# Retention and two MLPs in one launch: order of ScalarE's work in the opening, and the queue that reloads the low parts of x

## The chip, the cores and the metric

One core of a Trainium2 chip. The metric is the device time of one execution in microseconds (us), the median of the runs. TensorE is the matrix engine (PE in the profile's rows, PEld its weight loads), VectorE is DVE, ScalarE is ACT, GpSimd is POOL; SyncE (SP) has no arithmetic and only asks for transfers. ACTq and SPq in a row are these engines' sequencers asking for a transfer.

## What is computed

```python
# q, k, v: [4, 8, 768, 64]
for t in range(S):
    state = gamma * state + k[t] outer v[t]
    y[t] = scale * q[t] @ state
x = y as [3072, 512]
h = x @ w_in;  x = (h * cos(h)) @ w_out                 # first MLP, d_ff 2048
h = x @ w_in;  x = act(h) @ w_out                       # second MLP
```

act is h for h >= 1, 0 for h <= -1 and (h + 1)^2 / 4 between.

## The kernel before

All work is in one program whose instructions stand in the order written by hand: each engine runs its own in that order, and semaphores hold one engine for another. Every float operand of a matmul is split into a high part and a low part (names ending in h and l); a product is three matmuls: high by high, low by high, high by low.

The 3072 tokens are six blocks b of 512, d_ff is sixteen chunks j of 128. The first MLP goes in two passes: k=0 takes chunks 0 to 7 for all blocks, k=1 chunks 8 to 15. That makes 96 steps (k, b, j). In a step TensorE does `first` (L793: 12 matmuls, x by w_in, into a PSUM bank) and `second` of the step three before (L893: 12 matmuls, g by w_out). Between them stand, for each step, `Parts`: `rounded` on ScalarE (L842, into a tile r), `fraction` on VectorE (L847), `cosine` on ScalarE (L853), and, beside the next step's `rounded`, `product` on VectorE (L856), `high` on ScalarE (L861, gh) and `low` on VectorE (L869, gl). The sums of a block are copied into tiles `o` and stored to yT by SP (L925); these tiles `o` and the tiles r come out of one set of five.

**Weights are converted in between.** A class `Convert` takes a raw load of weights (raw<-in_w, L191, SP) through numbered stages: `one` and `two` on ScalarE (L204, L211: cf or f, and cs), `shift` and `sign` on VectorE (L223, L229), `four` on GpSimd (L238, the sum), `five` on ScalarE (L141: the high part wih, woh or whi), `six` on GpSimd (L144: the low part wil, wol). For the second MLP the results and sums of them (s, L287) go to DRAM as wp, by SP (L318). In the opening x and y in the code are lists of such conversions: x[1] makes wih and wil of chunk 1, y[1] woh and wol, x[2] the next wih.

**The opening.** While the attention of the first tokens still runs (`att`: scores L505, masks L575, decays of keys and queries L483 and L493, state updates L617 and L628, the output's parts `finish_high` L141 and `finish_low` L734), three steps of the first MLP are written out by hand in the function `opening(i, n)` (L1602), i = 0, 1, 2.

**x between the passes.** In pass 0 the parts of x are stored to DRAM (xTh, xTl). For pass 1 they are read back block by block into tiles xh and xl. `load_parts` (L762), called in the third step of the block before, writes down four pieces, two of xh and two of xl, 512 KB each; `fetch_x` (L771), called in every step between `first` and `second`, asks for up to two of the pieces, on SP. So xh is asked for in the step after `load_parts`, xl in the step after that; blocks b = 0 to 5 of pass 1 have four pieces each, 12 loads of xh and 12 of xl.

**Semaphores of transfers.** The transfers of SP and ScalarE share eight semaphores, DMAHW0 to DMAHW7, in turn; a transfer waits for the one that held its semaphore before. An engine that has come to a transfer that waits does nothing else until then.

## Time and profile before

| | us |
|---|---|
| median of three runs | 1064.48 (1064.04 to 1064.78) |
| the profiled execution, its own time | 1065.51 |
| its span, first to last instruction | 1063.7 |
| TensorE busy | 1054.7 |
| VectorE busy | 754.8 |
| ScalarE busy | 639.5 |
| GpSimd busy | 598.4 |

The mean granted TensorE clock is 0.999 of full speed. 1.8 us of the profiled execution lie outside its span. In the rows, a timeline's line joins neighbouring instructions of one kind (xcount): the first number is the start of the first, the second the time to the end of the last, and the bracket behind is the time for which the engine stood still before it and what ended that.

### The profile page before, as it was taken

To read this page: it belongs to the slowest core of one execution; us is meant where nothing else is said; L and a number is where in the kernel's file an instruction comes from. 1 tells how busy PE (TensorE), PEld (TensorE's weight loads), DVE (VectorE), ACT (ScalarE), POOL (GpSimd) and SP (SyncE) were. 2 spreads that over 40 slices of the span, in tenths; PEclk is the share of its full clock that TensorE was granted. 3 is DMA by queue.
4 is the path that set the end of the run, shared out by engine and by line. 5 is a ranking of instruction groups with operands and counts; after the bars stand their busy time and mean duration, and the time that the engine had idled before them with its cause. 6 is when DMAs were issued, how large, how long until landed. Compare 5 with 4: busy or idle time off the path is not lost.

```text
span 1063.7 us, 17827 instructions
## 1 busy us (share of the span) xinstructions
PE 1054.7 (99%) x6290; PEld 865.1 (81%) x6290; DVE 754.8 (71%) x1035; ACT 639.5 (60%) x1148; POOL 598.4 (56%) x520
## 2 busy tenths in 40 slices
PE   8999999999999999999999999999999999999998
PEld 6788888888888888888878888888888888888887
DVE  6858777887566446657475577778887787987875
ACT  4664344544366455657475677777667786666764
POOL 4844212221155377877885378965549885464550
PEclk9999999999999999999999999999999999999999
DMA  9697599898574699988988679898489899586642
GB/s 352 230 324 225 162 278 293 290 282 281 167 265 188 224 301 323 343 275 309 312 280 299 224 252 316 279 366 298 163 227 331 319 350 351 159 265 199 213 136 87
DMA packets 131705, 280.21 MB, mean 263 GB/s; under 512 B 14624, under 2 KB 41376, under 8 KB 131616
## 3 DMA queue, kind: packets, MB, share of 16 engines
q1 hardware_dynamic: 121968, 251.80, 70.6%
q10 hardware_dynamic: 9648, 27.27, 7.1%
q8 instruction: 50, 0.82, 0.3%
q14 instruction: 39, 0.32, 0.1%
HBM read 195.39 MB, written 83.62 MB: 262 GB/s over the span
## 4 chain that ended last, share of the span: by engine, by line
PE 84%; DMA 7%; POOL 4%; DVE 3%; issue 1%; ACT 1%; SPq 1%; POOLq 0%; ACTq 0%; DVEq 0%
PE b L1119 21%; PE y L1137 21%; PE b L893 19%; PE b L793 18%; DMA wp<-s 3%; PE b L661 2%; DMA yT<-o 1%; PE b L1253 1%; DMA qk<-in_qk 1%; POOL s L144 1%; PE b L537 1%; PE b L554 1%; DMA xl<-xTl 1%; POOL s L287 1%; DMA wp<-f 1%
## 5 line engine op out<-in xcount | busy, mean ns | idle before, releaser
L842 ACT ACTIVATE r<-b 128x512 int32<-128x512 f32 x96 | 56.8, 591 | 156.9 <-PE b L793 129.8
L847 DVE SCALAR_TENSOR_TENSOR r<-b,r 128x512 f32<-128x512 f32 x96 | 66.0, 687 | 109.6 <-ACT r L842 104.3
L1190 DVE TENSOR_TENSOR xh<-y,xh 128x1024 f32<-128x1024 f32 x86 | 105.1, 1222 | 30.6 <-PE y L1137 29.1
L238 POOL TENSOR_TENSOR cf<-cf,cs 128x512 int32<-128x512 int32 x40 | 51.6, 1290 | 131.9 <-DVE cf L229 93.9
L893 PE MATMUL b<-gh,wo 128*128 128x512 f32 x384 | 97.9, 389 | 0.0
L793 PE MATMUL b<-xh,wi 128*128 128x512 f32 x384 | 94.8, 389 | 0.0
L1310 POOL TENSOR_TENSOR ft<-r,f 128x512 f32<-128x512 f32 x23 | 29.8, 1296 | 114.1 <-PE y L1137 100.9
L1119 PE MATMUL b<-wih,wi 128*128 128x512 f32 x320 | 86.9, 389 | 0.0
L1190 DVE TENSOR_TENSOR xl<-y,xl 128x1024 f32<-128x1024 f32 x63 | 76.7, 1218 | 13.2 <-PE y L1137 13.2
L1137 PE MATMUL y<-gh,wo 128*128 128x512 f32 x276 | 85.0, 389 | 0.0
L893 PEld LDWEIGHTS b<-gh,wo 128*128 128x128 f32 x384 | 72.0, 188 | 15.2 <-ACT gh L861 0.2
L793 PEld LDWEIGHTS b<-xh,wi 128*128 128x128 f32 x384 | 72.1, 188 | 15.0
L893 PE MATMUL b<-gh,woh 128*128 128x512 f32 x192 | 76.9, 406 | 0.6 <-DVE xl L734 0.4
L861 ACT ACTIVATE gh<-b 128x512 fp32r<-128x512 f32 x96 | 57.0, 594 | 31.7 <-DVE b L856 31.5
L853 ACT ACTIVATE r<-r 128x512 f32<-128x512 f32 x96 | 60.7, 632 | 25.5 <-DVE r L847 25.3
L893 PE MATMUL b<-gh,wol 128*128 128x512 f32 x192 | 73.9, 390 | 0.0
L793 PE MATMUL b<-xh,wih 128*128 128x512 f32 x192 | 73.6, 396 | 0.2
L793 PE MATMUL b<-xh,wil 128*128 128x512 f32 x192 | 72.4, 390 | 0.0
L869 DVE TENSOR_TENSOR gl<-b,gh 128x512 fp32r<-128x512 f32 x96 | 65.7, 684 | 7.7 <-ACT gh L861 5.6
L1119 PEld LDWEIGHTS b<-wih,wi 128*128 128x128 f32 x320 | 60.0, 188 | 12.7 <-DVE gl L1162 0.3
L1137 PE MATMUL y<-wo,wo 128*128 128x512 f32 x276 | 70.0, 389 | 0.0
L1137 PE MATMUL y<-wi,wo 128*128 128x512 f32 x276 | 70.0, 389 | 0.0
(184 smaller groups left out, 2768.7 us busy)
## 6 DMA issues: line engine op xcount, KB each, us to landing
wi<-wp SPq DMA_DIRECT2D x66, 512.0 KB, 5.2
raw<-in_w SPq DMA_DIRECT2D x64, 512.0 KB, 6.6
wo<-wp SPq DMA_DIRECT2D x63, 512.0 KB, 5.5
wp<-whi SPq DMA_DIRECT2D x48, 256.0 KB, 4.3
wp<-s SPq DMA_DIRECT2D x32, 256.0 KB, 3.7
w<-cf ACTq DMA_DIRECT2D x26, 256.0 KB, 5.2
xTh<-xh ACTq DMA_DIRECT2D x12, 512.0 KB, 6.0
xTl<-xl ACTq DMA_DIRECT2D x12, 512.0 KB, 6.4
```

The lines of the kernel that those rows point to most:

```text
L238: nc.gpsimd.tensor_tensor(out=f, in0=f, in1=self.s, op=ALU.add)
L793: nc.tensor.matmul(out=h, lhsT=w[:, c * P:(c + 1) * P], rhs=x[:, c, :], start=(i == 0), stop=(i == len(terms) - 1),)
L842: nc.scalar.activation(out=self.r.bitcast(I32), in_=self.h, func=AF.Identity, scale=INV_2PI, bias=0.25)
L847: nc.vector.scalar_tensor_tensor(out=self.r, in0=self.h, scalar=INV_2PI, in1=self.r.bitcast(I32), op0=ALU.mult, op1=ALU.subtract,)
L853: nc.scalar.activation(out=self.r, in_=self.r, func=AF.Sin, scale=TWO_PI, bias=HALF_PI)
L861: nc.scalar.activation(out=self.gh, in_=self.h, func=AF.Copy)
L869: nc.vector.tensor_tensor(out=self.gl, in0=self.h, in1=self.gh.bitcast(F32), op=ALU.subtract)
L893: nc.tensor.matmul(out=acc[k, b][e], lhsT=w[:, s], rhs=g, start=(begin and i == 0), stop=(last and i == 2),)
L1119: nc.tensor.matmul(out=to, lhsT=w[:, c * P:(c + 1) * P], rhs=x, start=begin and n == 0, stop=n == len(terms) - 1, skip_group_check=not begin,)
L1137: nc.tensor.matmul(out=to[:, e, :], lhsT=w[:, e * P:(e + 1) * P], rhs=a, start=begin and m == 0, stop=m == 2, skip_group_check=not begin,)
L1190: nc.vector.tensor_tensor(out=a, in0=y, in1=a, op=ALU.add)
L1310: nc.gpsimd.tensor_tensor(out=o, in0=x, in1=z, op=ALU.subtract)
```

## The change

In `opening`, the second step (i = 1) makes gh of its chunk (`now.high`) and the first stage of y[1] before the high and low part of x[1]'s weights; the third step (i = 2) makes the high and low parts of y[1] before the second stage and the shift of x[2] and before `finish_low`. `load_parts` asks at once for the first two pieces (xh) on SP; the following step's `fetch_x` asks for the other two (xl) on ScalarE. Line numbers behind L768 are one higher in the changed kernel.

```diff
@@ -765,12 +765,13 @@
         for t, d in zip(xt[1, b], xT_d[b]):
             for c in range(0, NP, 2):
                 coming.append((t[:, c:c + 2, :].bitcast(F32), d[:, c:c + 2, :]))
+        fetch_x(nc.sync)
 
     coming = []
 
-    def fetch_x():
+    def fetch_x(eng):
         for t, d in coming[:2]:
-            nc.sync.dma_start(out=t, in_=d)
+            eng.dma_start(out=t, in_=d)
         del coming[:2]
 
     def load_part(b, es, eng=nc.sync):
@@ -1643,11 +1644,11 @@
                     now.cosine()
                     att.finish_low(n)
                     now.product()
+                    now.high()
+                    y[1].one()
                     x[1].five()
                     x[1].six()
-                    now.high()
                     now.low()
-                    y[1].one()
                     y[1].two()
                 else:
                     y[1].shift()
@@ -1664,11 +1665,11 @@
                     att.decay_k(n + 1)
                     att.finish_high(n)
                     now.cosine()
+                    y[1].five()
+                    y[1].six()
                     x[2].two()
                     x[2].shift()
                     att.finish_low(n)
-                    y[1].five()
-                    y[1].six()
                     now.product()
                     x[2].sign()
                     x[2].four()
@@ -1818,7 +1819,7 @@
                 now = l < NH - 1 if k == 0 else l != NH - 1 and (l != 3 or b > 2) or len(todo) > len(order2) - READY
                 conv.start(todo.pop(0) if todo and now else None, stage)
                 first(k, b, j, 4 + i % 4)
-                fetch_x()
+                fetch_x(nc.scalar)
                 send_parts()
                 done = second(i - LAG)
                 n = blocks.index((k, b)) + 1
```

ScalarE in the opening, second step, names of the code above: from the second step's cosine to the third step's `rounded`. Before:

```order
L853 ACTIVATE r<-r 128x512
L141 ACTIVATE wih_619<-cf 128x512
L861 ACTIVATE gh<-b_533 128x512
L204 ACTIVATE cf<-raw 128x512
L211 ACTIVATE cs<-raw 128x512
L842 ACTIVATE r<-b_635 128x512
```

With the change:

```order
L854 ACTIVATE r<-r 128x512
L862 ACTIVATE gh<-b_533 128x512
L204 ACTIVATE cf<-raw 128x512
L141 ACTIVATE wih_625<-cf 128x512
L211 ACTIVATE cs<-raw 128x512
L843 ACTIVATE r<-b_635 128x512
```

gh and the first stage of y[1] (cf) stand ahead of wih; its second stage (cs) stays behind.

ScalarE, third step, from its cosine to the next step's gh. Before:

```order
L853 ACTIVATE r<-r 128x512
L211 ACTIVATE cs<-raw 128x512
L141 ACTIVATE woh_732<-cf 128x512
L842 ACTIVATE r<-b_743 128x512
L141 ACTIVATE xh<-b_756 128x4x128
L861 ACTIVATE gh<-b_635 128x512
```

With the change:

```order
L854 ACTIVATE r<-r 128x512
L141 ACTIVATE woh_728<-cf 128x512
L211 ACTIVATE cs<-raw 128x512
L843 ACTIVATE r<-b_743 128x512
L141 ACTIVATE xh<-b_756 128x4x128
L862 ACTIVATE gh<-b_635 128x512
```

woh stands ahead of cs. The orders of VectorE, GpSimd and TensorE are as before; on GpSimd wil and wol are where they were.

SP in the step (1, 4, 11), the fourth of block 4 in pass 1, from the stores of s and whi behind the xh pair on; the brackets show the semaphores waited for (DMAHW are transfers). Before:

```order
L318 DMA wp_133<-s 128x512 [waits DMAHW2_49,Pool_49]
L318 DMA wp_133<-whi 128x512 [waits DMAHW3_49,Activation_49]
L318 DMA wp_134<-s 128x512 [waits DMAHW4_49,Pool_49]
L318 DMA wp_134<-whi 128x512 [waits DMAHW5_49,Activation_49]
L318 DMA wp_135<-f 128x256 [waits DMAHW6_49,Pool_49]
L318 DMA wp_135<-whi 128x256 [waits DMAHW7_49,Activation_49]
L318 DMA wp_132<-f 128x512 [waits DMAHW0_49,Pool_49]
L318 DMA wp_132<-whi 128x512 [waits DMAHW1_49,Activation_49]
L191 DMA raw<-in_w 128x1024 [waits DMAHW2_49,DVE_49]
L773 DMA xl<-xTl_68 128x1024 [waits DMAHW3_49,PE_49]
L773 DMA xl<-xTl_68 128x1024 [waits DMAHW4_49]
```

With the change, from the xh pair on:

```order
L774 DMA xh<-xTh_67 128x1024 [waits DMAHW7_49,PE_49]
L774 DMA xh<-xTh_67 128x1024 [waits DMAHW1_49]
L191 DMA raw<-in_w 128x1024 [waits DMAHW3_49]
L318 DMA wp_133<-s 128x512 [waits DMAHW4_49,Pool_49]
L318 DMA wp_133<-whi 128x512 [waits DMAHW5_49,Activation_49]
L318 DMA wp_134<-s 128x512 [waits DMAHW6_49,Pool_49]
L318 DMA wp_134<-whi 128x512 [waits DMAHW7_49,Activation_49]
L318 DMA wp_135<-f 128x256 [waits DMAHW0_49,Pool_49]
L318 DMA wp_135<-whi 128x256 [waits DMAHW1_49,Activation_49]
L318 DMA wp_132<-f 128x512 [waits DMAHW2_49,Pool_49]
```

The xh pair stands one load of weights earlier, and the xl pair is gone: it stood behind the wp stores and a load of weights. The store wp_132<-f waited for DMAHW0, that of the first xh load; now it waits for DMAHW2, as the transfer behind the second xl load, which holds it.

ScalarE at the same place. Before:

```order
L141 ACTIVATE whi<-f 128x256 [waits DMAHW7_49]
L141 ACTIVATE whi<-f 128x512 [waits DMAHW1_49]
L842 ACTIVATE r<-b_5928 128x512 [waits DMAHW3_49,PE_49]
L861 ACTIVATE gh<-b_5859 128x512 [waits DVE_49,Activation_49]
L853 ACTIVATE r<-r 128x512 [waits DVE_49]
```

With the change:

```order
L141 ACTIVATE whi<-f 128x512 [waits DMAHW1_49]
L774 DMA xl<-xTl_68 128x1024 [waits DMAHW0_49]
L774 DMA xl<-xTl_68 128x1024 [waits DMAHW2_49]
L843 ACTIVATE r<-b_5930 128x512 [waits DMAHW3_49,PE_49]
L862 ACTIVATE gh<-b_5859 128x512 [waits DVE_49,Activation_49]
L854 ACTIVATE r<-r 128x512 [waits DVE_49]
```

The two xl loads stand ahead of L842 (now L843). The first yT store (DMAHW3 in both) is waited for by L842 in both; the second xl load waits for DMAHW2, the raw load ahead of that store.

## Rows read from the trace of the kernel before

**Rows 1.** Page, part 1: busy us (share of the span) xinstructions, by engine

```profile
PE 1054.7 (99%) x6290; PEld 865.1 (81%) x6290; DVE 754.8 (71%) x1035; ACT 639.5 (60%) x1148; POOL 598.4 (56%) x520
```

**Rows 2.** Timeline, TensorE, opening: start us, us, engine line op out<-in xcount [idle<-releaser]

```profile
39.05 1.09 PE L679 MATMUL b<-w,v 128*64 128x128 f32 x16
40.21 0.69 PE L617 MATMUL b<-v,kd 128*64 128x64 f32 x16
41.25 1.17 PE L893 MATMUL b<-gh,woh 128*128 128x512 f32 x4 [0.35 <-DVE xl L734]
...
44.47 1.16 PE L505 MATMUL b<-qk 64*128 64x128 f32 x16 [0.21 <-PE b L893]
...
49.24 1.09 PE L679 MATMUL b<-w,v 128*64 128x128 f32 x16
50.16 0.63 PE L617 MATMUL b<-v,kd 128*64 128x64 f32 x16
51.03 1.19 PE L893 MATMUL b<-gh,woh 128*128 128x512 f32 x4 [0.24 <-ACT woh L141]
```

**Rows 3.** Timeline, ScalarE, opening

```profile
33.44 0.63 ACT L141 ACTIVATE wih<-cf 128x512 fp32r<-128x512 f32 x1 [2.09 <-POOL cf L238]
33.98 0.58 ACT L861 ACTIVATE gh<-b 128x512 fp32r<-128x512 f32 x1
```

**Rows 4.** Timeline, VectorE, opening

```profile
34.59 0.69 DVE L869 TENSOR_TENSOR gl<-b,gh 128x512 fp32r<-128x512 f32 x1 [2.51 <-ACT gh L861]
...
37.06 0.68 DVE L229 SCALAR_TENSOR_TENSOR cf<-raw,cf 128x512 int32<-128x512 int32 x1
...
41.62 1.26 DVE L229 SCALAR_TENSOR_TENSOR cf<-raw,cf 128x512 int32<-128x512 int32 x1
```

**Rows 5.** Timeline, GpSimd, opening

```profile
35.61 1.48 POOL L493 TENSOR_TENSOR kq<-qk,w 128x512 f32<-128x512 f32 x1
37.88 1.28 POOL L238 TENSOR_TENSOR cf<-cf,cs 128x512 int32<-128x512 int32 x1 [0.79 <-DVE cf L229]
...
41.05 1.28 POOL L144 TENSOR_TENSOR wol<-cf,woh 128x512 fp32r<-128x512 f32 x1 [0.90 <-ACT woh L141]
```

**Rows 6.** One line, L773: duration ns min/median/max, first and last start us

```profile
L773 SPq DMA_DIRECT2D xl<-xTl x12: 320/388/998, 306.0 to 540.1; - x12
```

**Rows 7.** Timeline, TensorE, 525 to 552 us

```profile
531.15 2.07 PE L893 MATMUL b<-gh,wo 128*128 128x512 f32 x8
...
539.40 1.98 PE L793 MATMUL b<-xh,wi 128*128 128x512 f32 x8
...
544.84 1.98 PE L793 MATMUL b<-xh,wi 128*128 128x512 f32 x8
...
548.04 0.73 PE L793 MATMUL b<-xl,wi 128*128 128x512 f32 x2 [0.50 <-DMA xl<-xTl]
...
551.35 0.84 PE L793 MATMUL b<-xh,wi 128*128 128x512 f32 x3
```

**Rows 8.** Timeline, ScalarE, 515 to 552 us

```profile
529.97 0.60 ACT L842 ACTIVATE r<-b 128x512 int32<-128x512 f32 x1 [7.38 <-DMA yT<-o]
530.46 0.59 ACT L861 ACTIVATE gh<-b 128x512 fp32r<-128x512 f32 x1
...
542.04 0.67 ACT L204 ACTIVATE f<-raw 128x512 f32<-128x512 f32 x1 [1.31 <-DMA wp<-f]
...
545.62 0.57 ACT L861 ACTIVATE gh<-b 128x512 fp32r<-128x512 f32 x1
...
551.47 0.60 ACT L861 ACTIVATE gh<-b 128x512 fp32r<-128x512 f32 x1 [2.24 <-DVE b L856]
```

**Rows 9.** Windows: each engine busy us (x), granted clock, DMA share, GB/s

```profile
534.00:542.00 8.00, 8.00 (x37) 6.63 (x36) 6.19 (x10) 4.53 (x8) 5.39 (x7) 1.00 1.03 380
```

**Rows 10.** Page, part 6, DMA issues: engine op xcount, KB each, us to landing

```profile
raw<-in_w SPq DMA_DIRECT2D x64, 512.0 KB, 6.6
...
xTl<-xl ACTq DMA_DIRECT2D x12, 512.0 KB, 6.4
```

## Prediction

> **What bounds the kernel now.** I read the page's busy times first, then TensorE's timeline of the opening, then the chain of waits backwards from the last block of the first MLP. TensorE is busy for 1054.7 us of a span of 1063.7 [rows 1]: only time in which TensorE stands still can be won, and an edit on another engine counts for what it takes from such a stall or puts there. The change touches two places with stalls, and the reader should look for both.
>
> The first is the opening. In TensorE's timeline L679 to L617 takes 40.21 − 39.05 = 1.16 us, the same pair undisturbed 50.16 − 49.24 = 0.92: 0.24 lost. Three rows print an idle time: 0.35 at 41.25, 0.21 at 44.47, 0.24 at 51.03 [rows 2]. Together 1.04 us. (Ends of matmuls are modelled, so a little more may be hidden; I add nothing for that.)
>
> The second is where block 5 of the pass k=1 starts. Two steps begin at 539.40 and 544.84, 5.44 apart, the next at 551.35, 6.51 later: 1.07 lost, and the row at 548.04 names the releaser, the load of xl [rows 7]. ScalarE is late there too: it stands still for 7.38 us until the store of yT has freed a tile, rounds at 529.97 (L842) and makes gh from 530.46 to 531.05 [rows 8], 0.10 before TensorE takes it at 531.15 [rows 7].
>
> A measurement of this kernel tells a change from none at about 0.2%, 2.1 us.
>
> **(a) second step: gh ahead of wih.** Nothing is added; two operations change places. ScalarE starts wih at 33.44, after 2.09 idle for GpSimd's sum, and gh at 33.98 behind it; the pitch of one operation is 33.98 − 33.44 = 0.54 [rows 3]. VectorE's gl starts at 34.59 after 2.51 idle, waiting for that gh [rows 4]: its product was done by 34.59 − 2.51 = 32.08. So gh can start at 32.1, 1.9 earlier, inside ScalarE's idle time, and wih still starts at 33.44 when its sum comes: the move itself costs nothing while both gh and the first half of y[1] (another 0.54) fit into the 31.35 to 33.44 in which ScalarE waits. gl is then some 1.8 earlier. What follows on VectorE are the shift of y[1], two masks that wait for TensorE's own scores, and the sign L229 at 37.06, 0.68 long [rows 4], which releases GpSimd's sum at 37.88 after 0.79 idle [rows 5]. From there come the decay of the keys that L617 takes at 40.21, and woh. How much of the 1.8 reaches L229? It would now run while GpSimd is in L493, 35.61 to 37.09 [rows 5]. A row shows what happens then: L229 at 41.62 takes 1.26 instead of 0.68 [rows 4] beside GpSimd's operation of 41.05 to 42.33 [rows 5], ending 0.55 after it. By that row the moved L229 ends at 37.64, 0.10 earlier than now; if it is not held, at 37.1 or before, 0.65 earlier. The bounds for (a) at L617 are thus 0.10 and the whole 0.24.
>
> **(b) third step: woh ahead of cs.** wol waits 0.90 for woh and starts at 41.05 [rows 5]. With cs behind it, woh comes one pitch, 0.54, earlier, plus what (a) gave. wol ends 0.54 earlier, and the L229 beside it (41.62 to 42.88 [rows 4]) ends earlier by as much, since it ended 0.55 after wol. Behind it on VectorE stands xl L734, which frees the banks at 41.25 and 44.47. (The row at 44.47 names the L893 that had run straight before it; I take VectorE's xl, the late one, for the cause.) cs is 0.54 later; its shift on VectorE has GpSimd's work ahead of it, so I cost it at nothing; if that cover is gone it costs at most 0.54 at L793 of the following step.
>
> Sum of the opening: 0.24 at 40.21, about 0.1 of the 0.35 at 41.25 (before L229), 0.21 at 44.47, 0.24 at 51.03 (woh, the same chain): **0.8**; bounds 0.25 (L229 held, only one stall goes) and 1.04.
>
> **(c) low parts on ScalarE's queue, a step earlier.** Twelve issues go from SP to ScalarE, 388 ns the median, 998 the longest [rows 6]: on SP nothing is gained that TensorE sees. In five of the six blocks the row of xl's line shows no wait of TensorE, and each puts two issues, 0.8 us, and what wait for a ring semaphore there is, on ScalarE ahead of L842; I cost it at nothing, covered by the three steps that lie between a step and the use of its gh. In the last block the loads, asked for until 540.1 [rows 6], are asked for when ScalarE gets to them, idle since 529.97 − 7.38 = 522.6 [rows 8], as the ring lets it: in the order rows the second load waits for a transfer asked for ahead of the yT store that L842 needs, so both are asked for before 530, ten us sooner. The stall of 1.07 goes: **−1.07**.
>
> What is late next? The bytes are the same, so what was asked for between 530 and 540 now lands behind them. In the order rows the store wp_132<-f stood ahead of both xl loads, and now stands behind them and waits for the second one's semaphore; and L204 on ScalarE waits for that store. That L204 is the one at 542.04, already 1.31 idle for it [rows 8]. The two loads are 2 x 0.52 MB; at the 380 GB/s of this stretch, where the queues are full (share 1.03) [rows 9], they take 2.8 us. Behind L204 on ScalarE everything follows back to back, so gh at 545.62 and gh at 551.47 [rows 8] come later by the same. Without the xl stall TensorE takes them half a step, 2.72, after the starts 544.84 and 550.28, at 547.56 and 553.00. They end now at 546.19 and 552.07: room of 1.37 and 0.93. A delay d costs max(0, d − 0.93). Bounds: d = 0 (the queue had room) and 3.1 (a tenth slower). I take 2.6, a little under the 380 GB/s row, as the earlier asking also fills moments in which SP was held: 2.6 − 0.93 = **+1.7**.
>
> And the 0.10 of room at 531.15: the yT stores are asked for before the xl loads. Loads of 512 KB land 6.6 us after SP asks, stores of the same size on ScalarE's queue 6.4 [rows 10]: neither queue is served first, so I take transfers in the order of asking and cost this at nothing; the bound is below, as a rival.
>
> Sum against the profiled execution: 1065.51 − 0.8 − 1.07 + 1.7 = 1065.3. That execution stands 1.03 above the median of the three runs, 1064.48, so the forecast is **1064.3**, no change that can be told.
>
> **The rivals.** *The xl stall is simply gone.* If the early loads fill time in which the queues had room, d stays under 0.93 and nothing takes the stall's place: 1064.48 − 0.8 − 1.07 = 1062.6, and with the whole opening 1062.4. For it: the stall is printed with its releaser, and ScalarE is idle for 7.38 us where it would ask. Against: a share of 1.03 over eight us [rows 9].
>
> *The opening gives little.* L229 runs beside L493 and the 1.8 us of gl end in 0.25 for TensorE: 1065.51 − 0.25 − 1.07 + 1.7 − 1.03 = 1064.9. For it: the 1.26 at 41.62 [rows 4].
>
> *Slower: the loads on ScalarE's queue hold the yT stores.* L842 at 529.97 waits for a store of yT. If ScalarE's queue is served in turn with SP's, whatever it asks for before 530 shares the engines with those stores: at worst both loads' 2.8 us go ahead of them, at half share 1.4. L842 and gh follow, and with 0.10 of room 2.7 reach TensorE; the later delay of 1.7 is then hidden in it. 1064.48 − 0.8 − 1.07 + 2.7 = 1065.3. It turns the change into a loss from a hold of 0.10 + 0.8 + 1.07 = 1.97 on. Against it: the equal landings [rows 10]; for it: no row shows a load on ScalarE's queue in so full a stretch. The Trainium skill, page "DMA: Bandwidth & Descriptors", section "Issuing engines are not separate DMA queues", says that transfers started by different engines run on the same 16 DMA engines and interleave, and that spreading them only saves issue time. By that rule this rival's 1065.3 would be nearer than my 1064.3.
>
> **How the numbers follow.** Forecast as summed, 0.50. Stall simply gone 0.27: the mechanism is sure, its cover not; about half of these cases, with most of the opening won, pass 0.2%. Opening little 0.12. ScalarE's queue holding the stores 0.11; with a poor opening as well (1065.9) or a longer hold some of it passes 0.2%. The range must leave out no more than 2 in 10: from 1062.3 (stall gone, opening whole) to 1065.6 (stores held, opening at 0.5). Faster by over 0.2% (under 1062.35) 0.13, within 0.82, slower (over 1066.6) 0.05.
>
> **What would show it.** In the opening: gh at about 32.1, gl by 33, wih at 33.4 still; L229 of y[1] ending at 37.1 to 37.6; woh, wol and the stalls at 41.25, 44.47 and 51.03 shorter, TensorE 0.8 earlier by 52. In the last block of pass 1: xl asked for before 530 on ScalarE's queue, no wait of TensorE for xl; L204 near 542 waiting about 2.6 longer for wp<-f, and TensorE waiting for gh near 548 and 553. If that wait is missing, the second case holds; if the first gh after 530 is late and TensorE waits at 531, the last. I am wrong outright if TensorE's stalls elsewhere change by over a microsecond, or if the opening gets slower.

## The result: 1074.2 us, slower by 1 in 100, and the profile after

| | us |
|---|---|
| before, median of five runs | 1064.48 (1063.78 to 1064.78) |
| changed, median of five runs | 1074.20 (1073.68 to 1075.79) |
| ratio, with its interval | 1.0096 (1.0082 to 1.0111) |
| changed, the profiled execution and its span | 1075.38, 1073.6 |

The forecast was 1064.3, within 1062.3 to 1065.6. The change costs 9.7 us. The two profiled executions differ by 1075.38 − 1065.51 = 9.87, and that is what the following accounts for. The mean granted clock is 0.998 against 0.999; where that difference arises is told under "The clock at block 2". One execution of e2 below (1167.46 us at a granted clock of 0.85) and one of the kernel before in e1's session (4916.8 us) are slow ones and left out.

The page of the changed kernel: TensorE's busy time against [rows 1], and the costliest group of L894 (before: L893) in part 5, whose last field is the idle time ahead of it.

```profile
PE 1059.8 (99%) x6290; PEld 865.1 (81%) x6290; DVE 752.7 (70%) x1035; ACT 640.2 (60%) x1148; POOL 598.0 (56%) x520
...
L894 PE MATMUL b<-gh,wo 128*128 128x512 f32 x384 | 101.9, 396 | 6.9 <-DVE o L919 4.6
```

Matmuls that start late are also modelled longer, and a few ran at half the clock, so part of the loss stands here as busy time, 1059.8 for 1054.7; the rest is idle time in front of L894, the `second` matmuls, and its releaser is new: VectorE's line L919. The view of waits by engine (waited for: us in total, times, longest us) of the changed kernel says the same for TensorE and for its weight loads:

```profile
PE b L894 <- DVE o L919: 4.6, 7, 2.1
PE b L894 <- ACT whi L141: 1.1, 1, 1.1
...
PEld b L894 <- DVE o L919: 8.9, 11, 2.6
```

Neither of the waits for L919 is in that view of the kernel before. L919 is the copy of a block's finished sums out of the PSUM banks (`evacuate`): at the start of each block `second` begins new sums in the same four banks, and so has to wait until they are empty.

Where this happens, in TensorE's timeline of the changed kernel:

```profile
40.01 0.69 PE L617 MATMUL b<-v,kd 128*64 128x64 f32 x16
40.62 1.20 PE L894 MATMUL b<-gh,woh 128*128 128x512 f32 x4
...
49.95 1.19 PE L894 MATMUL b<-gh,woh 128*128 128x512 f32 x4 [0.16 <-ACT woh L141]
...
345.69 1.16 PE L894 MATMUL b<-gh,wo 128*128 128x512 f32 x4 [0.37 <-ACT gh L862]
347.56 1.20 PE L894 MATMUL b<-gh,wo 128*128 128x512 f32 x4 [0.71 <-DVE o L921]
...
435.07 0.70 PE L894 MATMUL b<-gh,wo 128*128 128x512 f32 x2 [1.07 <-ACT whi L141]
437.90 0.74 PE L894 MATMUL b<-gh,wo 128*128 128x512 f32 x2 [2.13 <-DVE o L919]
439.10 2.07 PE L894 MATMUL b<-gh,wo 128*128 128x512 f32 x4 [0.46 <-DVE o L919]
...
540.93 2.11 PE L894 MATMUL b<-gh,wo 128*128 128x512 f32 x8 [0.19 <-ACT gh L862]
...
549.24 1.98 PE L794 MATMUL b<-xh,wi 128*128 128x512 f32 x8
```

The reader should lay such a timeline beside that of before and subtract the starts of the same matmuls. L617 is at 40.01 for 40.21 and the woh matmuls at 49.95 for 51.03 [rows 2]; the same xh matmuls of `first` are at 549.24 for 539.40 [rows 7], 9.84 late. The difference only jumps at a few places:

| place (times of the changed kernel) | step, us | late after it, us |
|---|---|---|
| opening (−1.09 at 52, −1.03 from 300 on) | −1.03 | −1.03 |
| first `second` of block 0 of pass 1, 345 to 348 | +1.63 | +0.60 |
| of block 2, 435 to 439 | +5.82 | +6.42 |
| of block 3, 484 to 485 | +1.54 | +7.96 |
| of block 4, 529 to 530 | +1.47 | +9.43 |
| 541 | +0.41 | +9.84 |
| the old stall for xl, near 560 | −1.07 | +8.77 |
| first `second` of block 5, 574 to 575 | +1.12 | +9.89 |

So the opening and the stall for xl went as the change means them to. 11.58 us come in at the starts of five of the six blocks of pass 1.

**The clock at block 2.** Windows of the changed kernel, of which the second number is TensorE's busy time and the number behind POOL's the granted clock:

```profile
436.00:438.00 2.00, 0.10 (x1) 0.10 (x1) 1.45 (x3) 0.52 (x2) 2.00 (x3) 1.00 0.54 221
438.00:440.00 2.00, 1.54 (x4) 1.00 (x5) 1.93 (x4) 1.52 (x3) 2.00 (x4) 0.63 0.88 329
440.00:442.00 2.00, 2.00 (x6) 1.52 (x6) 1.97 (x3) 0.26 (x1) 1.31 (x3) 0.52 1.02 359
```

TensorE is busy for 0.10 of 2 us between 436 and 438, as it waits for the banks. Behind that its clock falls to the lower of its two levels (1.2 for 2.4 GHz), and it is back at 1.00 in the window from 442 to 444. In between matmuls start 0.43 us apart in place of 0.23. From 439.10 on TensorE's lateness grows by 1.46 us; at the same matmuls in the profile of e5 below, where the clock stays at 1.00, it grows by 0.27. So about 1.2 of the 5.82 us are not waits: they are what the lower clock cost behind them. The same fall stands at block 2 in the profiles of e3, e10, e15 and e16 and at block 5 in that of e18; in those of e5, e9 and e11 there is none.

**The chain at block 2.** ScalarE's timeline of the changed kernel, with its sequencer's asks (ACTq):

```profile
32.02 0.60 ACT L862 ACTIVATE gh<-b 128x512 fp32r<-128x512 f32 x1 [0.77 <-DVE b L857]
...
33.35 0.63 ACT L141 ACTIVATE wih<-cf 128x512 fp32r<-128x512 f32 x1 [0.15 <-POOL cf L238]
...
393.17 0.93 ACTq L774 DMA_DIRECT2D xl<-xTl  x2
...
421.04 0.33 ACTq L781 DMA_DIRECT2D xh<-yp  x1
421.41 0.67 ACT L204 ACTIVATE f<-raw 128x512 f32<-128x512 f32 x1 [4.05 <-DMA wp<-whi]
...
429.20 0.33 ACTq L781 DMA_DIRECT2D xh<-yp  x1
429.57 0.67 ACT L204 ACTIVATE f<-raw 128x512 f32<-128x512 f32 x1 [2.98 <-DMA wp<-whi]
```

and the same of the kernel before:

```profile
413.82 0.33 ACTq L780 DMA_DIRECT2D xh<-yp  x1
414.20 0.67 ACT L204 ACTIVATE f<-raw 128x512 f32<-128x512 f32 x1 [0.48 <-DMA wp<-whi]
...
420.25 0.33 ACTq L780 DMA_DIRECT2D xh<-yp  x1
421.77 0.67 ACT L204 ACTIVATE f<-raw 128x512 f32<-128x512 f32 x1 [1.78 <-DMA raw<-in_w]
```

L781 (before: L780) is `load_part`, which brings the sums of pass 0 (yp) back for `evacuate`, in two transfers a block, and ScalarE asks for both. The change does not touch it, yet it stands 7.22 and 8.95 later. The bracket of the L204 behind it says on what: ScalarE stood still because a store of whi had not landed, and the L781 ahead of the L204 is what waits for it. (The raw load that the second L204 reads had landed at 427.80, so the ask for yp held it 1.4 us longer than its own input.) VectorE of the changed kernel follows:

```profile
430.27 0.73 DVE L223 TENSOR_SCALAR f<-f 128x512 int32<-128x512 int32 x1 [3.52 <-ACT f L204]
...
434.24 0.68 DVE L919 TENSOR_TENSOR o<-b,xh 128x512 f32<-128x512 f32 x1
436.56 0.69 DVE L870 TENSOR_TENSOR gl<-b,gh 128x512 fp32r<-128x512 f32 x1 [1.64 <-ACT gh L862]
437.16 0.68 DVE L919 TENSOR_TENSOR o<-b,xh 128x512 f32<-128x512 f32 x1
```

VectorE waits 3.52 for that L204 and does everything in its order behind it, the copies o at 434.24 and 437.16 too, and TensorE takes the banks after them (435.07 and 437.90 in its timeline above). The row at 435.07 names ScalarE's whi, which these matmuls (b<-gh,wo) do not read; the weight load ahead of it waits for VectorE's semaphore until 434.96, and the copy of 434.24 ends at 434.92, so I put this wait down to the copy. In the kernel before the first of these copies waited for TensorE instead, and the copies were through by 432.4, before TensorE came for the banks at 433.23. VectorE, and then TensorE, before:

```profile
428.67 0.69 DVE L918 TENSOR_TENSOR o<-b,xh 128x512 f32<-128x512 f32 x1 [2.01 <-PE b L893]
...
431.07 1.28 DVE L918 TENSOR_TENSOR o<-b,xh 128x512 f32<-128x512 f32 x2
```

```profile
433.23 1.98 PE L893 MATMUL b<-gh,wo 128*128 128x512 f32 x8
```

What is late ahead of this is GpSimd's work, whose inputs are the loads f<-w. GpSimd of the changed kernel, and then of the kernel before:

```profile
410.93 1.43 POOL L287 TENSOR_TENSOR s<-f 128x256 f32<-128x256 f32 x2 [10.42 <-DMA f<-w]
```

```profile
405.43 1.44 POOL L287 TENSOR_TENSOR s<-f 128x256 f32<-128x256 f32 x2 [7.11 <-DMA f<-w]
```

The load of f<-w is asked for by SP in both, at 406.35 for 400.61, and the two xl loads were behind it (SP, 402.27) and are now ahead of it (ScalarE, 393.17). From ask to landing f<-w takes 4.5 us now and took 4.8 before: the load itself is no slower, its ask is late. SP of the changed kernel:

```profile
404.02 0.32 SPq L318 DMA_DIRECT2D wp<-whi  x1
...
406.35 0.37 SPq L196 DMA_DIRECT2D f<-w  x1
```

The store at 404.02 waits for the semaphore that the second xl load holds, asked for by ScalarE at 393.56 and landed at 403.95. f<-w waits for a store that SP asked for at 397.46 and that landed at 406.33, and the asks between wait in the same way. So xl, asked for early, holds SP at its asks through the eight shared semaphores, although SP no longer asks for it.

Two causes can thus lie in the 5.8 us, and the experiments were made to hold them apart: xl goes ahead of what the conversions wait for (its bytes, and its places among the semaphores), and the unmoved yp loads wait for other transfers than before.

### The profile page after: what moved, and what is told of

Its sections match the earlier page's. It is cut to its first block, busy times and chain, and to the rows that moved or that the text cites. A ratio compares the mean times of both kernels' runs of the same rounds, so it can differ in the third digit from the quotient of the medians.

```text
span 1073.6 us, 17824 instructions
## 1 busy us (share of the span) xinstructions
PE 1059.8 (99%) x6290; PEld 865.1 (81%) x6290; DVE 752.7 (70%) x1035; ACT 640.2 (60%) x1148; POOL 598.0 (56%) x520
## 4 chain that ended last, share of the span: by engine, by line
PE 73%; DMA 9%; POOL 6%; DVE 4%; ACT 4%; issue 2%; SPq 1%; ACTq 0%; DVEq 0%; POOLq 0%
PE b L1120 21%; PE y L1138 20%; PE b L894 14%; PE b L794 12%; POOL s L144 2%; DMA yT<-o 2%; PE b L661 2%; DMA raw<-in_w 1%; DMA wp<-s 1%; POOL s L287 1%; POOL f L144 1%; DMA f<-w 1%; PE b L1254 1%; ACT whi L141 1%; DMA wp<-whi 1%
## 5 line engine op out<-in xcount | busy, mean ns | idle before, releaser
L843 ACT ACTIVATE r<-b 128x512 int32<-128x512 f32 x96 | 56.8, 591 | 149.5 <-PE b L794 115.6
L894 PE MATMUL b<-gh,wo 128*128 128x512 f32 x384 | 101.9, 396 | 6.9 <-DVE o L919 4.6
L894 PEld LDWEIGHTS b<-gh,wo 128*128 128x128 f32 x384 | 71.3, 189 | 26.9 <-DVE o L919 8.9
L894 PE MATMUL b<-gh,woh 128*128 128x512 f32 x192 | 76.9, 406 | 0.2 <-ACT woh L141 0.2
L894 PE MATMUL b<-gh,wol 128*128 128x512 f32 x192 | 74.0, 390 | 0.0
```

The lines of the kernel that those rows point to most:

```text
L843: nc.scalar.activation(out=self.r.bitcast(I32), in_=self.h, func=AF.Identity, scale=INV_2PI, bias=0.25)
L894: nc.tensor.matmul(out=acc[k, b][e], lhsT=w[:, s], rhs=g, start=(begin and i == 0), stop=(last and i == 2),)
```

## The experiments

Each diff is against the changed kernel (its own line left out where only the place is told). Theories: the loss is the opening's; it is that of xh asked for early; it is ScalarE standing at the ask; it is the place of xl's bytes in the order in which transfers are asked for; it is the turn of the yp loads. All ratios are against runs of the kernel before in the same session (its medians 1064.38 to 1064.78). Differences of TensorE's start times are taken as in the table above, from one profiled execution each.

### Which part: e1, e12

**e1**: parts (a) and (b) alone, the fetch as before.

```diff
-        fetch_x(nc.sync)
...
-                fetch_x(nc.scalar)
+                fetch_x(nc.sync)
```

> Only the opening's edit (a, b); the loads of x as in the kernel before. TensorE's starts in the changed kernel are 1.03 us earlier from 52 to 340 us. All theories on the loads (bytes, hold, xh) expect the same here: 1064.48 - 1.0 = 1063.5, TensorE's last stall (xl, 1.07) still there. If the opening were to cost something later, over 1064.5.

1063.51 us, ratio 0.9997 (0.9988 to 1.0007). The loss is gone: it belongs to part (c), all of it. The median is 0.87 below that of before in the session, the size forecast for the opening, though the interval holds no change too.

**e12**: part (a) alone; in the third step `y[1].five()` and `six()` are put back behind `finish_low`, the fetch is as before.

> The kernel before with the second step's edit (a) alone. By the prediction (a) gives 0.10 to 0.24 at 40.21 and (b) most of the 0.8: TensorE 0.1 to 0.5 us earlier by 52 us, 1064.0 to 1064.4. If (a) carries the opening: 0.8 to 1.1 earlier, 1063.4 to 1063.7.

One execution: 1064.32 us; behind the opening TensorE is 0.05 to 0.17 earlier than in the profile of before. In the seventeen profiles compared of kernels that have both (a) and (b), it is 0.37 to 1.40 earlier in the middle of pass 0, the middle one of them 1.05 (e1 0.79). The single execution of (a) lies under that spread: that (b), or both together, bring the larger part is likely, not shown.

### Which part of the fetch: e2, e11, e3, e4

**e2** and **e11** are one kernel: both pairs asked for as early as in the change, all by SP. e11 is a single execution, made for its trace.

```diff
-                fetch_x(nc.scalar)
+                fetch_x(nc.sync)
```

> The changed kernel with both pairs asked for early, but all on SP: ScalarE asks for none of them. Theory bytes (what is asked for early pushes the raw and w32 loads that the conversions wait for, whichever engine asks): 1070 to 1075, POOL still waiting long for f<-w near 405 us. Theory hold (ScalarE stands at its two asks and all its work behind them is late): 1063.5 or a little under, as no engine but SP is held. Theory xh (the xh pair ahead of a raw load does it alone): 1070 to 1075.

> The kernel of the run early_sp once more, for its trace (1066.2 in the median there): theory order expects f<-w32_1_5_0 to land less than 4 late, or TensorE's loss of 2.7 to lie at the starts of blocks, where ScalarE's evacuations are awaited.

e2: 1065.98 us in its ten executions, 1.0016 (1.0007 to 1.0025). e11: 1065.90. So being a step earlier costs some 2.5 us against e1, not 10; and none of the theories' numbers came out. In e11 f<-w is again asked for late, at 404.36, and takes 4.5 us to land.

**e3**: the old steps, but xl asked for by ScalarE.

```diff
-        fetch_x(nc.sync)
...
-                fetch_x(nc.scalar)
+                fetch_x(nc.scalar if len(coming) == 2 else nc.sync)
```

> The opening's edit; xh on SP and xl in the step of the kernel before, but xl on ScalarE's queue. Theory bytes: about that of the opening alone, 1063.5 to 1064.5. Theory hold: most of the loss is back, 1068 to 1074, ScalarE idle ahead of L843 in five blocks. Theory xh: 1063.5.

1072.51 us, 1.0075 (1.0062 to 1.0088): nearly the whole loss without the earlier step, and far over what the theory of the bytes expected. By its number the run speaks for ScalarE's standing at the ask, which e6 tests by itself. Why a later step helps so little, ScalarE's timeline of e3 shows, beside SP's of the kernel before:

```profile
391.72 3.82 ACTq L773 DMA_DIRECT2D xl<-xTl  x2
```

```profile
400.61 1.08 SPq L196 DMA_DIRECT2D f<-w  x1
...
402.27 0.92 SPq L773 DMA_DIRECT2D xl<-xTl  x2
```

In the same step of the program ScalarE gets to the ask 10.55 us sooner than SP does. SP has the stores of converted weights ahead of it, each of which waits for the engine that makes it and for its semaphore; so "a step earlier" was two steps in time more than the text of the change tells.

**e4**: xh early on SP as in the change, xl on SP in its old step.

```diff
-                fetch_x(nc.scalar)
+                if l != LAG:
+                    fetch_x(nc.sync)
```

> The opening's edit; all loads on SP; the xh pair early as in the changed kernel, the xl pair in the step of the kernel before. Theory xh: 1070 to 1075. Theory bytes: between, 1064 to 1067, as one pair of 1 MB in place of two goes ahead of the raw loads. Theory hold: 1063.5.

1063.87 us, 0.9997 (0.9988 to 1.0005): xh asked for early costs nothing that can be told. What remains is xl on ScalarE's queue. (The profiled execution of e4 is 1.83 above this median and loses 2.4 us between 430 and 545: a loss of that size in a single profile need not be the kernel's.)

### Standing at the ask, or passing others: e6, e5

**e6**: transfers of 4 KB in ScalarE's place, the whole of xl on SP in its old step.

```diff
-        fetch_x(nc.sync)
+        tiny.extend(coming[2:])
...
-                fetch_x(nc.scalar)
+                for t, d in tiny:
+                    nc.scalar.dma_start(out=t[:, :1, :8], in_=d[:, :1, :8])
+                tiny.clear()
+                fetch_x(nc.sync)
```

> The opening's edit and all loads on SP as before; in the place where the changed kernel asks for the two xl loads on ScalarE it asks for two transfers of 4 KB into the same tiles (xl is loaded in full by SP behind them). ScalarE waits for the same tiles and for its turn of the ring, but moves no bytes. Theory hold: 1069 to 1074. Theory jump: 1063 to 1065.5, two more places in the ring of eight included.

1065.22 us, 1.0010 (0.9998 to 1.0022). In its profile TensorE loses 2.18 at the start of block 0 and nothing at blocks 1 to 5. TensorE of e6:

```profile
345.84 1.17 PE L894 MATMUL b<-gh,wo 128*128 128x512 f32 x4 [0.91 <-ACT gh L862]
347.71 1.20 PE L894 MATMUL b<-gh,wo 128*128 128x512 f32 x4 [0.70 <-DVE o L921]
```

These are the two rows of the changed kernel at 345.69 and 347.56 over again. So the 1.6 of block 0 comes with asks on ScalarE's queue, however few their bytes; what in them delays it was not traced. The loss of the other blocks did not come with such asks, nor with the two places that they take among the semaphores, without the bytes.

**e5**: xl by ScalarE two steps later still.

```diff
-        fetch_x(nc.sync)
...
-                fetch_x(nc.scalar)
+                if len(coming) == 4:
+                    fetch_x(nc.sync)
+                elif l == LAG + 2:
+                    fetch_x(nc.scalar)
```

> The opening's edit; xh on SP as before; xl on ScalarE's queue, but two steps after the step in which the changed kernel asks, so at about the time at which SP gets to it in the kernel before (402 us for block 2). Theory jump (ScalarE's queue has no backlog, so its xl loads pass the raw and w32 loads that SP has yet to ask for, and the conversions wait for those): 1063 to 1065.5, the time of the opening alone. Theory hold (ScalarE standing at its asks is the cost): 1068 to 1074.

1071.17 us, 1.0058 (1.0044 to 1.0072); by its number it fits ScalarE's standing, too, and I had expected it to be faster. The asks moved to 399.85 and 401.92; f<-w was asked for at 401.20, nearly as before, but took 8.0 us to land in place of 4.8: GpSimd's L287 starts at 409.37 (before 405.43, changed 410.93). The move was too short to bring the order of before back, so the run is no test of it; e9 is.

### Which block: e7, e8, e10

**e7** takes the changed way for block 5 only, **e8** the same with both pairs on SP.

```diff
-        fetch_x(nc.sync)
+        if b == NB - 1:
+            fetch_x(nc.sync)
...
-                fetch_x(nc.scalar)
+                fetch_x(nc.scalar if (k, b) == (1, NB - 2) else nc.sync)
```

> The opening's edit, and the changed kernel's way of loading x for block 5 only; blocks 0 to 4 as before. By the prediction's own step for this place: 1063.5 - 1.07 + 1.7 = 1064.1. If the stall is simply gone: 1062.4. Theory jump allows either (the wp stores wait here, not a raw load); theory hold over 1065.

> As the last, but block 5's xl pair is asked for early on SP, behind its xh pair and ahead of the wp stores: no engine but SP can be held. All theories: the xl stall of 1.07 gone, and the wp stores later by up to 2.8: 1062.4 to 1064.1.

1064.23 us, 0.9994 (0.9985 to 1.0002), and 1064.26 us, 0.9991 (0.9982 to 1.0000). In both profiles TensorE no longer waits for xl, and loses 1.16 and 1.14 at the first `second` of block 5, at 563 to 566 of their own time. The place that the change was made for is worth nothing: what it frees is given back one block start later. The medians lie 0.4 below before, where the opening alone has 0.87.

**e10**: the changed way for block 2 only.

```diff
-        fetch_x(nc.sync)
+        if b == 2:
+            fetch_x(nc.sync)
...
-                fetch_x(nc.scalar)
+                fetch_x(nc.scalar if (k, b) == (1, 1) else nc.sync)
```

> The opening's edit, and the changed kernel's way of loading x for block 2 only. Theory order: the wait of TensorE at the start of that block (435 to 439 us, 5.8 in the changed kernel) is there without the others: f<-w32_1_5_0 lands 4 to 5 later, TensorE loses 3.5 to 5.8 at 433 to 439, 1066.5 to 1069.5 in all. If the loss needs the lateness from blocks 0 and 1: under 1065.5.

1070.21 us, 1.0045 (1.0034 to 1.0056), a little more than expected. TensorE of e10 (its `second` is L895, the copies L920):

```profile
433.66 0.70 PE L895 MATMUL b<-gh,wo 128*128 128x512 f32 x2 [0.86 <-ACT whi L141]
436.49 0.74 PE L895 MATMUL b<-gh,wo 128*128 128x512 f32 x2 [2.13 <-DVE o L920]
437.69 2.08 PE L895 MATMUL b<-gh,wo 128*128 128x512 f32 x4 [0.46 <-DVE o L920]
```

The same three waits as in the changed kernel, and a loss of 5.73 for its 5.82 (some 1.3 of it the lower clock again), with the loads of all other blocks as before. Block 2's loss is its own, not handed on from earlier blocks.

### The turn of the yp loads: e9, e14, e15, and their controls

That the yp loads wait for others than before can be seen in the order of the program, without a run. ScalarE's asks for yp ahead of block 2, before and with the change (the brackets show the semaphore waited for):

```
L780 DMA xh<-yp_76 128x1024 [waits DMAHW4_49]
L780 DMA xh<-yp_76 128x1024 [waits DMAHW2_49]

L781 DMA xh<-yp_76 128x1024 [waits DMAHW6_49]
L781 DMA xh<-yp_76 128x1024 [waits DMAHW7_49]
```

As SP and ScalarE take the eight semaphores in turn, two transfers moved from one to the other shift the turns of all that come between. Traced to the transfers, the second yp load waited before for a store that SP asked for at 415.46 and that landed at 420.23, and now for one asked for at 423.43 that lands at 429.18, 0.02 before ScalarE's ask.

**e9**: xl of blocks 1 to 4 by ScalarE, but three steps later, behind f<-w; blocks 0 and 5 on SP.

```diff
-        fetch_x(nc.sync)
...
-                fetch_x(nc.scalar)
+                if len(coming) == 4 or k == 0 or b >= NB - 2:
+                    fetch_x(nc.sync)
+                elif l == LAG + 3:
+                    fetch_x(nc.scalar)
```

> The opening's edit; x of blocks 0 and 5 loaded as before, xl of blocks 1 to 4 on ScalarE's queue, three steps after the step in which the changed kernel asks: for block 2 near 406 us, behind the load f<-w32_1_5_0 (asked for at 400.6 in the kernel before) and the raw load behind it (401.8). Theory order (what counts is only that xl, 1 MB, is asked for ahead of those loads; the run with two steps passed them by a microsecond): 1063.0 to 1064.5, POOL's s<-f of that block near 405 us again. If a load on ScalarE's queue costs by itself: over 1067.

1066.54 us, 1.0014 (1.0002 to 1.0026). GpSimd and ScalarE of e9:

```profile
405.14 1.44 POOL L287 TENSOR_TENSOR s<-f 128x256 f32<-128x256 f32 x2 [7.34 <-DMA f<-w]
```

```profile
424.46 0.33 ACTq L780 DMA_DIRECT2D xh<-yp  x1
424.84 0.66 ACT L204 ACTIVATE f<-raw 128x512 f32<-128x512 f32 x1 [3.91 <-DMA wp<-whi]
```

GpSimd is at its old time again, and most of the loss is gone, though not down to the 1063.0 to 1064.5 expected. But the second yp load still stands at 424.46 for 420.25, and TensorE loses 1.34, 1.26 and 1.86 at blocks 2, 3 and 4 of the profiled execution, which is 1.46 above the median.

**e14** is e9 with the second yp load asked for by SP, **e13** its control, e1 with the same.

```diff
-                    fill.append(lambda b=b: load_part(b - 1, range(2, NP), nc.scalar))
+                    fill.append(lambda b=b: load_part(b - 1, range(2, NP), nc.sync))
```

> The run act_behind (1066.5: xl of blocks 1 to 4 on ScalarE's queue, behind f<-w) with that load of yp on SP. Theory ring (ScalarE stands at L780 for a transfer that SP asks for six places later): the 3 us over the opening alone go, within 1 us of the control. If a load on ScalarE's queue costs otherwise: 1066 to 1067.

> Control: the opening's edit alone, with the second load of yp of each block (L780 in the first step) asked for by SP in place of ScalarE. All theories: about the opening alone, 1063 to 1065.

e13: 1063.70 us, 0.9994 (0.9985 to 1.0003): moving that load costs nothing by itself. e14: 1065.32 us, 1.0011 (1.0001 to 1.0020). In the profile of e14 the losses at blocks 2, 3 and 4 are gone: TensorE stays 0.69 to 0.85 ahead of before from the opening to the middle of block 4. TensorE of e14 at the start of block 2, without a wait:

```profile
432.54 1.98 PE L893 MATMUL b<-gh,wo 128*128 128x512 f32 x8
```

So the yp load's turn on ScalarE carries what was left in the profile of e9, some 1.3 to 1.9 a block. In the medians the excess over the control falls from 1066.54 − 1063.51 − (1064.69 − 1064.38) = 2.7 to 1065.32 − 1063.70 = 1.6, less than the profiles say, and short of the 1 us over the control that was expected. The profile of e14 has the stall for xl in block 5 (1.35 of idle time at 547.84) and that of the control has not, which makes 1.65 us between these two; whether that is the other 1.6 of the medians is not shown.

**e15**: the changed kernel with the second yp load on SP (the diff of e14 alone).

> The changed kernel with that load of yp on SP. Theory ring: the part of the loss that is ScalarE's stand at L780 goes, the part of the bytes ahead of f<-w stays: from 1074.2 to 1066 to 1069. If the ring plays no part: 1073 to 1075.

1075.52 us, 1.0102 (1.0081 to 1.0123): a miss, it is no better than the changed kernel. Its profiled execution, at 1072.30 its fastest, has no loss at blocks 3 and 4, but all of it, 5.75, at block 2, 1.4 at block 0 and 1.7 at block 5. At block 2 the first yp load, still on ScalarE, is the one that waits:

```profile
420.80 0.33 ACTq L781 DMA_DIRECT2D xh<-yp  x1
421.17 0.67 ACT L204 ACTIVATE f<-raw 128x512 f32<-128x512 f32 x1 [4.45 <-DMA wp<-f]
```

That is the changed kernel's row at 421.41 again: what it waits for is a store of weights that is itself late, because GpSimd's inputs were.

**e18** moves both yp loads to SP in the changed kernel, **e16** both in e10, **e17** both in e1.

> The changed kernel with both loads of yp on SP. Theory ring: 2 to 4.5 over the control, the bytes ahead of f<-w and block 0's 1.6. If the ring plays no part: 9 to 11 over the control.

> The run block2 (1070.2: the changed kernel's way of loading x for block 2 only) with both loads of yp of each block on SP, so that ScalarE asks for nothing else in pass 1. Theory ring: only the part of the bytes ahead of f<-w is left, 1.5 to 2.5 over the control. If ScalarE's stands at the loads of yp play no part at block 2: 5 to 7 over the control.

> Control: the opening's edit alone, with both loads of yp of each block on SP: 1063.5 to 1066, as SP gets to them later than ScalarE.

e17: 1064.62 us, 0.9995 (0.9983 to 1.0007). e18: 1072.47 us, 1.0072 (1.0057 to 1.0087), 7.85 over its control and between the two expectations. In its profile blocks 3 and 4 lose nothing and block 2 3.14 for 5.82, but block 5 loses 4.5 for 1.12, with the lower clock behind it: at both blocks the copies o wait for yp itself, which SP asks for late. e16: 1070.47 us, 1.0049 (1.0034 to 1.0064), a miss: it is no faster than e10. VectorE of e16 says why:

```profile
433.45 0.69 DVE L920 TENSOR_TENSOR o<-b,xh 128x512 f32<-128x512 f32 x1 [3.21 <-DMA xh<-yp]
```

ScalarE stands for yp no longer, but SP comes to the loads so late (427.13 and 428.54) that the copies wait for yp itself. Its loss of 6.94 at block 2 also holds more of the lower clock than that of e10: the granted clock is 0.50 from 436 to 442. The run put one wait in the place of another, and tells nothing on whether the first was the cause.

### What stays open

Block 2's 5.8 has two parts that were each measured alone there: xl ahead of f<-w (e11, loss 1.76; GpSimd's L287 at 408.88) and the turn of the yp loads (e9, loss 1.34). Together they make 5.73 (e10), not 3.1. Some 1.3 us of that is the lower clock, which e9 and e11 do not have. For the rest, argued, not shown: it is the lateness that adds. The last L204 ahead of the block's copies stands at 421.77 before, 424.84 in e9, 425.84 in e11 and 428.47 in e10: 3.07 and 4.07 late alone, 6.70 together, and the room that VectorE had before its copies were needed is used up only once. With the clock taken off, the losses of e11 and e10 fit that: 2.63 us more lateness, 3.97 − 1.3 = 2.7 more loss. These are single profiles; e16 was to test it and did not. The 1.12 at block 5 has no experiment beyond e7 and e8, which show the same.

## Why the prediction was wrong

**The step that failed** is the one sentence of part (c) on "five of the six blocks": two issues, 0.8 us, and a ring wait, "I cost it at nothing, covered by the three steps that lie between a step and the use of its gh". It holds for gh, and TensorE hardly waits for gh in these blocks. But gh is not the only thing that TensorE takes from behind ScalarE: at each block start it takes emptied banks, from VectorE, behind VectorE's share of the conversions, behind ScalarE's L204. That path has its own room (at block 2 the copies were through by 432.4 for banks wanted from 433.23 on), and I had not looked it up. It measured 11.58 us in five blocks in place of 0, about 1.2 of it the lower clock behind the longest wait. And a ring wait was named there, but only for the transfers that move. The unmoved ones wait too: SP's stores and f<-w behind the xl loads, and the yp loads, whose turns change; the order of the program shows both without a run.

**The same bytes, another order.** I took transfers in the order of asking, and applied it in the last block alone, to the store wp_132<-f. In the changed kernel the transfers asked for between 390.5 and 407.6 do land in that order. But f<-w, which lands at 410.87 for 405.37 before, is late because it is asked for late, behind stores that wait for the semaphores of the xl loads. The question what the early loads hold up had to be put for all six blocks, to everything that SP asked for in the ten us by which ScalarE is sooner. The Trainium skill, page "DMA: Bandwidth & Descriptors", section "Issuing engines are not separate DMA queues", says that spreading transfers over engines saves issue time alone. For the service the traces agree that nothing is gained: block 2's xl loads take 6.9 and 10.4 us from ask to landing on ScalarE's queue, 6.8 and 7.5 before on SP's. But e3 and e2 are 6.5 us apart with the same transfers, by when the asking engine gets to its ask and what then stands behind it.

**The opening, −0.8: right as far as can be told.** −1.03 in the profile, −0.87 in the medians (e1), where the interval holds no change too. gh at 32.02 for the 32.1 forecast, wih still at 33.35; the sign L229 of y[1] started 0.13 before GpSimd's L493 and ended at 36.37, earlier than the 37.1 to 37.6 forecast, as I had missed that it passes in front; L493 took 1.75 for 1.48. VectorE, and then GpSimd, of the changed kernel:

```profile
35.64 0.73 DVE L229 SCALAR_TENSOR_TENSOR cf<-raw,cf 128x512 int32<-128x512 int32 x1
```

```profile
35.77 1.75 POOL L493 TENSOR_TENSOR kq<-qk,w 128x512 f32<-128x512 f32 x1
```

L617 came 0.20 earlier, within the bounds 0.10 and 0.24; e12, with (a) alone, gave 0.05 to 0.17.

**The xl stall, −1.07: gone as forecast, but oversized.** xl was asked for at 536.69, 9.4 us late like all else, so at 527.3 of the old clock, "before 530". But the stall is not in every execution: of six profiles in which block 5's loads stand as before and TensorE is not late, three have it (before 1.07, e1 and e14), three do not (e12, e13, e17). TensorE of e1 and of e12 at the same place:

```profile
548.33 0.72 PE L793 MATMUL b<-xl,wi 128*128 128x512 f32 x2 [1.42 <-DMA xl<-xTl]
```

```profile
546.40 1.07 PE L793 MATMUL b<-xl,wi 128*128 128x512 f32 x4
```

The profiled execution of before was 1.03 above the median, and I took its stall for the median's. Where an execution has no such stall, 1.07 of the gain of 1.87 was not there to be won; how many have it is not known.

**The new wait for the store wp_132<-f, +1.7: there, but mis-sized and covered.** The L204 that stood at 542.04 before is this one:

```profile
552.49 0.67 ACT L204 ACTIVATE f<-raw 128x512 f32<-128x512 f32 x1 [2.01 <-DMA wp<-whi]
```

It waits 2.01 for 1.31. The row names wp<-whi; the semaphore is that of wp_132<-f, asked for at 547.66 and landed at 552.47. It is 10.45 later than before, where TensorE is 9.84 later: 0.6 in place of the 2.6 that I took for the delay d, and under the room of 0.93. The two gh behind it end at 556.65 and 562.11, TensorE takes them at 557.40 and 562.84, and no delay reaches it. What took the stall's place is the wait for the banks at block 5's start, 1.12 (1.16 and 1.14 in e7 and e8). That this is near the 1.7 is luck.

**The rivals.** None of them is what happened. Of the slower one, loads holding the yT stores, there is a trace at the place that it names, but not of its size: the first yT store takes 5.0 us to land for 4.6 before, and TensorE waits for the gh behind it (540.93 in its timeline), 0.41 in the table in place of 2.7. ScalarE's own wait for yT is no longer, 6.45 for 7.38 [rows 8]; whether the xl loads slowed the store is not shown. The prediction's last sentence, that stalls elsewhere would make it wrong outright, names the case; it should have been a rival with a price.

## What to carry to other kernels

Before a piece of work off the critical engine is costed at nothing, list everything that the critical engine takes from behind it, not only the next operand: buffers to be emptied, once a block, can have less room than the operands of every step (here 0.8 us at block 2, from 432.4 to 433.23). A stall can also cost more than its own length, as here the clock fell behind the longest one. And when a transfer is moved to another engine's queue, ask three things: when that engine gets to the ask, which transfers now wait for its semaphore, and which unmoved transfers change their turn. If you want the gain of this change, take (a) and (b) alone (1063.51 us, not told from before by its interval) and leave the low parts of x on SP.

## What was not expected of the hardware

An ask on ScalarE's queue came 10.55 us sooner than on SP's for the same step (391.72 in e3 against 402.27), as SP's sequencer works through its own list of waiting stores. Transfers landed nearly in the order in which they were asked for, across both queues. What an early load delayed was mostly the asking of others: f<-w landed 3.4 to 5.5 us later than before (408.81 in e11, 410.87 in the changed kernel, 405.37 before), with 4.5 us from ask to landing for 4.8. An engine that waits at an ask for another's transfer to give back a semaphore is held to within 0.02 us of that landing: 429.18 and 429.20. And TensorE's granted clock fell to 1.2 GHz inside the kernel, behind a wait in which it was busy for 0.10 of 2 us, and cost about 1.2 us.
